# A tensor of its own for each block sum that stands in PSUM, and a new order for the late work

## The chip, the cores and the metric

The kernel runs on one core of a Trainium2 chip. The metric is the device time of one execution in microseconds (us), as the median of the runs. Five engines work side by side: TensorE (PE in the profile, its weight loads PEld), VectorE (DVE), ScalarE (ACT), GpSimd (POOL) and SyncE (SP), whose queue issues all the transfers. Matrix products land in PSUM, which has eight banks of 512 fp32 values in each of 128 partitions.

## What is computed

A linear attention (4 batches, 8 heads, 768 steps, head width 48) feeds a gated MLP, all in fp32:

```
state = w_t * state + k_t v_t^T ;  y_t = r_t (state + u k_t v_t^T)        # attention, one step
h = gelu(y @ w_in) ;  u, v = halves of h (512 columns each)
v_n = layer norm of v, times g_ln
v_s = w_sg @ v_n + b_sg                # w_sg mixes the 768 positions of one batch
out = y + (u * v_s) @ w_out
```

## The kernel before

Attention runs in chunks of 128 steps, 6 to a batch and 24 in all (steps `n`); the MLP follows each batch. Every fp32 product of the MLP is three matmuls of high and low parts (`mm3_part` at L1049 to L1051; `mm3_more` at L1243 adds three more to a sum that is already there).

**The order.** Nothing is ordered by hand. Each piece of work is a Python generator that yields one `Op` for each engine instruction or group, with an estimate of its time in us, what it waits for and which buffers it takes. `Plan.run` lists them: it takes, engine by engine, the operation that can start first by these estimates, and among those within a tolerance the one of the lowest rank. The ranks come from constants and from the tables `SHIFT` and `LEAN`, found by a search. So estimates and tables do nothing on the chip by themselves; they set the order of the instructions on every engine, and the engines run their instructions in that order. The framework below adds the semaphore waits, from the tensors that each instruction reads and writes. The planner's own model has no waits of that kind between two sums in one tensor.

**The last batch.** Its mixing `w_sg @ v_n` (two halves of positions by six blocks of 128) is done with fewer products by sums and differences of blocks. `value_sums`, `early_sums` and `late_sums` make the sums of operands on DVE, ACT and POOL. The products run in `first_sum`, `second_sum` and `third_sum`, each for `j` = 0 and 1 (128 columns each):

- `second_sum(j)` accumulates three blocks, and DVE reads the running sum between them: block 2 (operands `kt`, `winh`, `winl`), then `u2[j] = ps + p1` (L1287); block 3 (`x`, `winl`, `winh`), then `p15[j] = ps + p15` (L1295); block 4 (`x`, `winh`, `winl`), then L1304, then the gate.
- `third_sum(j)` accumulates its first block, DVE makes `p15[j]` from it (L1324), then the second block, L1335, then the gate.
- `gated` is the gate: multiply-add (L1144) and multiply by `u` (L1146) on DVE, both in place in PSUM, the high part on ACT (L1148), the low part on DVE (L1150). The `g` that it makes is an operand of `out_piece`, whose result DVE adds to the input (L1357) and SP stores.

PSUM has `a_ps` (one tensor of two banks), `y_ps` (one tensor of two banks), and four tensors of one bank each, `m_ps` three times and `resets`, which all the other MLP products take in turn. Both sums of `second_sum` stand in `a_ps`, one bank each, and both of `third_sum` in `y_ps`.

As fillers for ACT there are checks of the inputs: `f64_check` (L1437 load, L1440 and L1441) and twelve `range_check` (load of 516 KB at L694, L697, L699). The verdict on them (L1364 to L1381) sets a flag which is read at the end.

Of the kernel before, what the change touches and what calls it, by code (L numbers as in the profile page):

```python
# [29 lines left out]
HALF = S // 2  # L30
# [17 lines left out]
    "f64_check": {0: 6.13524, 1: -1.25073, 2: 2.58709, 3: 21.0265, 4: 1.86039, 5: -5.70527, 6: -3.22829,  # L48
        7: -4.72882, 8: -32.5565, 9: -75.5317},
    "range_check": {0: -10.8008, 1: -9.83328, 2: 25.8484, 3: -12.1442, 4: 14.1794, 5: -6.94772, 6: -6.75246,  # L50
        7: -4.37133, 8: -8.93084, 9: -6.04386, 10: 18.5049, 11: 4.47546},
# [6 lines left out]
        21: 2.56083, 22: 6.50075, 23: 0.926434},  # L58
# [3 lines left out]
        21: -3.66692, 22: 4.4884, 23: -0.122174},  # L62
# [5 lines left out]
        15: -3.39515, 16: -0.550587, 17: 3.40935, 18: 3.60141, 19: 1.63861, 20: 2.50708, 21: 2.31902, 22: -7.3781,  # L68
# [8 lines left out]
        21: 1.1852, 22: -6.40664, 23: -32.7259},  # L77
    "state": {0: 1.6156, 1: -1.5654, 2: -0.151852, 4: -1.00713, 5: -1.43132, 6: 0.0152658, 7: 0.148255,
        8: -4.14956, 9: -1.43419, 10: -1.96613, 11: -1.55185, 12: -0.134183, 13: -1.23942, 14: -0.0105872,
        15: -7.76325, 16: 1.22982, 17: -6.96928, 18: -2.43314, 19: 0.638084, 20: 1.35566, 21: 2.77548,  # L80
        22: 0.936183, 23: -15.5807},
    "taken": {0: -0.262701, 1: 2.39625, 2: -1.14432, 3: 0.217207, 4: 1.06527, 5: 5.92211, 6: -2.94535, 7: -2.95988,
        8: 5.10548, 9: 8.1973, 10: 6.2663, 11: 5.18081, 12: 4.46058, 13: 4.60809, 14: 1.43792, 15: -5.39583,
        16: -2.06968, 17: -1.47464, 18: -1.78307, 19: -1.09584, 20: 8.6431, 21: 6.51443, 22: 27.2314, 23: 7.25823},
# [15 lines left out]
        16: -11.6337, 17: -2.93257, 18: 15.7862, 19: -3.68233},  # L100
# [4 lines left out]
        7: 5.08266, 8: 1.08435, 9: 2.39182, 10: 0.696228, 11: 5.4523, 12: 2.68057, 13: -5.5209, 14: -10.064,  # L105
        15: -14.4952, 16: -13.7637, 17: -65.3122},
    "turned_copy": {0: -0.00376847, 1: 2.08601, 2: 2.36332, 3: 4.99214, 4: 0.358231, 5: 3.23889, 6: -8.60673,
        7: 3.02214, 8: -5.60305, 9: -3.76615, 10: -9.9281, 11: -11.0889, 12: 2.86951, 13: -2.39513, 14: -2.09959,
        15: 44.1632},
    "move": {0: 5.13594, 1: -0.550027, 2: 1.01544, 3: 7.61938, 4: 7.77121, 5: -1.87103, 6: -1.63015, 7: -5.38766,  # L110
        8: 5.01974, 9: -17.0269, 10: 7.95121, 11: 38.0365},
    "split_x": {0: -5.87337, 1: -1.21064, 3: -3.08211, 4: -1.59682, 5: 2.46398, 6: 5.39234, 7: 13.1576, 8: 1.09464,
        9: -6.79638, 10: 10.9691, 11: 6.13701, 12: 15.758, 13: -0.387358, 14: -1.71503, 15: -2.57609, 16: -3.23669,
        17: 3.48517, 18: -19.4792, 19: -1.84619, 20: -47.5863, 21: -27.2088, 22: -25.5326, 23: -14.1693},
    "v_piece": {0: 0.974425, 1: 0.0770227, 2: 0.0252557, 3: -0.26627, 4: -2.79717, 5: -1.99287, 6: -3.35885,
        7: 0.760898, 8: -0.0152414, 9: -0.145742, 10: 0.648668, 11: -6.73745, 12: -2.61262, 13: -2.01732,
        14: 0.737588, 15: -0.200081, 16: -0.36828, 17: -2.1716, 18: 10.1152, 19: -26.4527, 20: -3.15993,
        21: -43.5842, 22: -48.7493, 23: -14.1388},
    "u_piece": {0: -0.43406, 1: -0.156609, 2: 0.407676, 3: -0.0686205, 4: 6.03383, 5: 7.87225, 6: 7.83671,
# [4 lines left out]
    "gate_piece": {0: 0.415732, 1: 0.510674, 2: -1.60287, 3: -1.12889, 4: -0.911901, 5: -1.67499, 6: 0.685951,  # L124
        7: 3.55094, 8: -6.13281, 9: -4.24099, 10: -5.33866, 11: -4.05245, 12: -5.07821, 13: -0.422561, 14: 7.83702,
        15: 8.75934, 16: 0.209474, 17: -1.31632, 18: -3.60713, 19: 1.03, 20: 4.65649, 21: 1.95126, 22: -15.4408,
        23: 17.0337},
    "out_piece": {0: -5.70279, 1: 1.7949, 2: -1.59687, 3: -2.24862, 4: -1.98186, 5: -11.7889, 6: -5.01684,
        7: 0.480244, 8: 0.181361, 9: 0.421304, 10: 0.100822, 11: 2.08585, 12: -10.0637, 13: -23.9868, 14: -5.74609,
        15: 10.0572, 16: -9.94732, 17: 14.3604, 18: 10.6945, 19: 14.5855, 20: -52.8156, 21: -22.494, 22: -13.0148,  # L130
        23: -8.57544},
    "value_sums": {0: -31.4738, 1: 52.068, 2: -53.6573},
    "early_sums": {0: 7.43323, 1: 0.307297, 2: 7.17974},
    "late_sums": {0: 1.94387, 1: 8.12424, 2: -0.928206},
    "first_sum": {0: -18.2786, 1: 8.1141},
    "second_sum": {0: -74.8167, 1: -1.83379},
    "second_gate": {0: -33.8644, 1: 4.67722},
    "third_sum": {0: -5.77672, 1: 6.70228},
    "verdict": {0: 22.9598},
# [14 lines left out]
        21: 0.422507, 22: 0.0982615, 23: -0.259888},  # L154
# [11 lines left out]
    "v_piece": {1: 0.806915, 2: 0.321106, 5: 0.907102, 6: 0.197632, 7: 0.0545095, 8: 0.39416, 10: -0.0275803,
        11: 0.185728, 13: -0.159257, 14: 0.0198662, 15: 0.248228, 16: -0.238145, 17: 0.159771, 18: -0.0597079,
        19: 0.689192, 21: 0.210592, 22: 0.128118},
    "value_sums": {0: 0.0241681, 2: -0.282933},
    "early_sums": {0: 0.249284},  # L170
    "late_sums": {1: -0.0420833},
# [61 lines left out]
class Event:  # L233
    t = None
# [230 lines left out]
def rwkv_gmlp(ctx: ExitStack, tc: tile.TileContext, wpad, kr, vtok, ktok, vt, u, ucol, w_in, consts_, w_sgT, w_out, out):  # L465
    nc = tc.nc
# [24 lines left out]
    per, ps = pool("per", 1), pool("ps", 1, space=PSUM)  # L491
# [17 lines left out]
    s_kr = slots("KR", 4, [2 * NP * C + T])  # L509
# [5 lines left out]
    s_a = slots("a", 3, [2, NP, T])  # L515
# [108 lines left out]
    def dma(kb, **kw):  # L624
        return Op({"SP": 0.62 if kb in (16, 48) else 0.47}, kb=kb, **kw)
# [529 lines left out]
    sums = Part("y", "z")  # L1155
# [57 lines left out]
    whole = {"DVE": 0.48, "POOL": 1.0}  # L1213
# [37 lines left out]
    def first_sum(j):  # L1251
# [9 lines left out]
        op = yield Op({"ACT": 0.42, "DVE": 0.47}, take=[s_y3], done=sums.e_p1[j])  # L1261
# [13 lines left out]
    def second_sum(j):  # L1275

        for s in range(TH):
            op = yield Op({"PE": 0.53}, after=[sums.e_b[2, s], sums.e_a[2, s], *([sums.e_y] if j and s == 0 else [])],
                          take=[] if s or j else [m_a], done=sums.e_y if s == 0 and j == 0 else None)
            if s == 0 and j == 0:  # L1280
                sums.y, = op.got
                sums.y.n = 2
            ps = sums.y.tile[:, j, :HALF]
            mm3_part(ps, (columns_of(sums.b[2, s], j), sums.a[2, s]), s, TH)
        op = yield Op({"DVE": 0.5}, after=[sums.e_p1[j]], take=[s_a], done=sums.e_u2[j])
# [6 lines left out]
        op = yield Op({"DVE": 0.5}, after=[sums.e_p15[j]], take=[s_g], done=sums.e_c22[j])  # L1292
# [433 lines left out]
```

## Time and profile before

| | us |
|---|---|
| median of 3 runs | 359.95 (359.12 to 360.01) |
| the profiled execution | 361.06, its span 359.3 |
| PE busy in the span | 345.6 (96%) |
| DVE / ACT / POOL busy | 281.6 / 226.9 / 122.5 |
| mean granted clock of TensorE | 0.997 |

The profile comes from one execution. Its span runs from the first to the last instruction; 1.76 us of that execution's time lie around it. A matmul's row begins where it is issued and its end is modelled, so that successive matmuls overlap in the rows; the distance between their starts says how fast PE goes.

### The profile page before, as it was taken

How to read it: one execution, taken by the hardware profiler on the slowest of the kernel's cores; microseconds unless marked ns; L12 is line 12 of the kernel's file. 1: busy time of each engine (PE TensorE's matmuls, PEld its weight loads, DVE VectorE, ACT ScalarE, POOL GpSimd, SP SyncE). 2: the span in 40 equal slices, each digit the busy share in tenths (PEclk: the TensorE clock that was granted, in tenths of full speed). 3: DMA queues.
4: the chain of work that ended last, by engine and by line, in shares of the span. 5: the costliest groups of instructions: out<-in, count | busy, mean ns of one | idle time of the engine just before them, and what ended most of it. 6: DMA issues, size and time to landing. Idle time of an engine off the chain costs nothing.

```text
span 359.3 us, 11044 instructions
## 1 busy us (share of the span) xinstructions
PE 345.6 (96%) x4459; PEld 315.3 (88%) x4459; DVE 281.6 (78%) x550; ACT 226.9 (63%) x602; POOL 122.5 (34%) x206
## 2 busy tenths in 40 slices
PE   8999998999999999999999999999999999999892
PEld 7785776899999889899999999899999898998782
DVE  7999989989989898979989893446554468787582
ACT  2869977973455558765325557724137899888960
POOL 8240544333244543443335524321012243144000
PEclk9999999999999999999999999999999999999998
DMA  7989886521365756435476630013347655746602
GB/s 271 374 287 294 273 284 220 165 84 44 112 192 174 229 150 208 141 122 162 130 218 203 183 102 2 0 68 111 102 122 247 235 178 165 234 163 189 203 32 70
DMA packets 28422, 60.56 MB, mean 169 GB/s; under 512 B 3408, under 2 KB 13136, under 8 KB 28368
## 3 DMA queue, kind: packets, MB, share of 16 engines
q1 hardware_dynamic: 28368, 59.82, 51.8%
q8 instruction: 36, 0.59, 0.7%
q14 instruction: 18, 0.15, 0.1%
HBM read 53.91 MB, written 4.72 MB: 163 GB/s over the span
## 4 chain that ended last, share of the span: by engine, by line
PE 79%; DVE 4%; ACT 4%; DMA 2%; issue 1%; SPq 1%; POOL 0%; ACTq 0%; DVEq 0%
PE m_ps L1049 15%; PE m_ps L1050 14%; PE m_ps L1051 14%; PE resets L1049 6%; PE resets L1050 5%; PE resets L1051 5%; PE a_ps L773 4%; PE y_ps L796 3%; PE y_ps L807 3%; DMA x<-y 2%; PE y_ps L780 2%; PE a_ps L1243 2%; PE m_ps L1243 1%; PE y_ps L1243 1%; SPq L1017 1%
## 5 line engine op out<-in xcount | busy, mean ns | idle before, releaser
L1049 PE MATMUL m_ps<-wsgh,vn 128*128 128x384 f32 x114 | 39.3, 345 | 0.0
L1051 PE MATMUL m_ps<-wsgh,vn 128*128 128x384 f32 x114 | 38.6, 338 | 0.0
L1050 PE MATMUL m_ps<-wsgl,vn 128*128 128x384 f32 x114 | 38.5, 338 | 0.0
L748 ACT ACTIVATE a<-KR,own 128x64 f32<-128x64 f32 x136 | 34.4, 339 | 2.9 <-DVE own L742 2.8
L472 ACT COPY x<-y_ps 128x384 f32<-128x384 f32 x23 | 11.0, 476 | 31.2 <-PE y_ps L796 27.0
L739 POOL TENSOR_TENSOR RK<-RK 128x384 f32<-128x384 f32 x16 | 17.2, 1074 | 24.7 <-DVE W L683 6.1
L1049 PE MATMUL m_ps<-xT,winh 128*128 128x384 f32 x72 | 25.4, 353 | 0.0
L1050 PE MATMUL m_ps<-xT,winh 128*128 128x384 f32 x72 | 24.4, 339 | 0.0
L1051 PE MATMUL m_ps<-xT,winl 128*128 128x384 f32 x72 | 24.4, 338 | 0.0
L1050 PE MATMUL m_ps<-g,wouth 128*128 128x384 f32 x68 | 23.2, 341 | 0.4 <-DVE g L1150 0.4
L1101 DVE TENSOR_TENSOR vn<-v,vn 128x512 fp32r<-128x512 f32 x21 | 15.2, 729 | 10.4 <-ACT vn L472 9.6
L1049 PE MATMUL m_ps<-g,wouth 128*128 128x384 f32 x68 | 23.2, 342 | 0.0
L1051 PE MATMUL m_ps<-g,woutl 128*128 128x384 f32 x68 | 23.0, 338 | 0.0
L1148 ACT CAST g<-m_ps 128x384 fp32r<-128x384 f32 x20 | 9.5, 475 | 21.1 <-DVE m_ps L1146 21.1
L773 PE MATMUL a_ps<-KR 64*64 64x128 f32 (+1 forms) x768 | 22.4, 252 | 0.4 <-POOL KR L685 0.2
L1049 PE MATMUL m_ps<-winh,xT 128*128 128x512 f32 x54 | 22.0, 407 | 0.0
L1049 PEld LDWEIGHTS m_ps<-wsgh,vn 128*128 128x128 f32 x114 | 21.4, 188 | 0.6
L1050 PEld LDWEIGHTS m_ps<-wsgl,vn 128*128 128x128 f32 x114 | 21.5, 188 | 0.1
L796 PE MATMUL y_ps<-a,vtok 64*64 64x64 f32 x768 | 21.4, 224 | 0.1
L1051 PEld LDWEIGHTS m_ps<-wsgh,vn 128*128 128x128 f32 x114 | 21.5, 188 | 0.0
L1051 PE MATMUL m_ps<-winh,xT 128*128 128x512 f32 x54 | 21.4, 397 | 0.0
L1050 PE MATMUL m_ps<-winl,xT 128*128 128x512 f32 x54 | 21.4, 396 | 0.0
(321 smaller groups left out, 1103.0 us busy)
## 6 DMA issues: line engine op xcount, KB each, us to landing
KR<-in_kr SPq DMA_DIRECT2D x24, 512.0 KB, 5.0
RK<-in_ktok SPq DMA_DIRECT2D x20, 384.0 KB, 4.0
W<-in_wpad SPq DMA_DIRECT2D x24, 260.5 KB, 3.3
KR<-in_wpad SPq DMA_DIRECT2D x12, 521.0 KB, 3.6
vtok<-in_vtok SPq DMA_DIRECT2D x24, 192.0 KB, 4.3
out<-o SPq DMA_DIRECT2D x21, 192.0 KB, 3.1
vn<-in_w_in SPq DMA_DIRECT2D x6, 512.0 KB, 6.3
KR<-in_w_in SPq DMA_DIRECT2D x6, 512.0 KB, 5.1
```

The costliest lines, as they stand in the source:

```text
L472: nc.scalar.copy(o, i) if e == "ACT" else engine[e].tensor_copy(o, i)
L739: engine[op.e].tensor_tensor(t[:, 1], t[:, 1], t[:, 0], ALU.mult)
L748: nc.scalar.activation(a[:, j, p], eyes, AF.Copy, scale=o[:, j, p:p + 1])
L773: nc.tensor.matmul(ps_[64 * c_:64 * c_ + 64, j, p * C:p * C + (2 * T if c_ < turn else T)], x.K[rows, at:at + T], r_, start=True, stop=True)
L796: m = nc.tensor.matmul(place(y, j, q, r, c_), x.V[64 * c_:64 * c_ + 64, h * D - up(p, j):h * D - up(p, j) + 64], x.a.tile[64 * c_:64 * c_ ...
L807: m = behind(m, nc.tensor.matmul(place(y, j, q, r, c_), S2.tile[64 * j:64 * j + 64, 16 + 64 * p - up(p, j):80 + 64 * p - up(p, j)], x.R[64 ...
L1049: nc.tensor.matmul(ps, lh, rh, start=(i == 0), stop=False)
L1050: nc.tensor.matmul(ps, lh, rl, start=False, stop=False)
L1051: nc.tensor.matmul(ps, ll, rh, start=False, stop=(i == n - 1))
L1101: engine[op.e].tensor_tensor(vn.tile[:, 1], v, vh.bitcast(F32), ALU.subtract)
L1148: nc.scalar.copy(gh, ps)
L1243: nc.tensor.matmul(ps, x, y, start=False, stop=True, skip_group_check=True)
```

## The change

`second_sum(0)` keeps `a_ps`, of which it uses one bank; `second_sum(1)` takes `y_ps` for itself. `third_sum(j)` takes one of the four one-bank tensors for each `j`. The events that told the second sum that the first had taken the tensor are gone. The estimates of the operations behind the last batch are set to traced durations. The load of the first three range checks is split in two transfers of 258 KB. `SHIFT` and `LEAN` have new values for the late pieces: those of the checks, of the attention chunks from about n = 20 on, and of the MLP pieces of the last one and a half batches. The products, the casts and the additions are the same and as many.

```
-    "first_sum": {0: -18.2786, 1: 8.1141},
-    "second_sum": {0: -74.8167, 1: -1.83379},
-    "second_gate": {0: -33.8644, 1: 4.67722},
-    "third_sum": {0: -5.77672, 1: 6.70228},
-    "verdict": {0: 22.9598},
+    "first_sum": {0: 1.73604, 1: 10.2119},
+    "second_sum": {0: -94.3654, 1: 16.5429},
+    "second_gate": {0: -60.8972, 1: 32.2017},
+    "third_sum": {0: -18.3163, 1: 8.56913},
+    "verdict": {0: 79.1124},
...
     def range_check(n):
-        op = yield dma(516, take=[s_kr], after=[ch[N - 1].e_k])
+        two = n < 6
+        op = yield dma(258 if two else 516, take=[s_kr], after=[ch[N - 1].e_k], apart=two)
...
-        nc.sync.dma_start(t, wpad[b, g:g + 2].rearrange("a p x -> p a x"))
+        if two:
+            nc.sync.dma_start(t[:, 0], wpad[b, g])
+            yield dma(258)
+            nc.sync.dma_start(t[:, 1], wpad[b, g + 1])
+        else:
+            nc.sync.dma_start(t, wpad[b, g:g + 2].rearrange("a p x -> p a x"))
...
     def gated(h_, half, d, m, g, ps, ready=None, j=0):
-        yield Op({"DVE": 0.54}, after=[e_u, h_.e_u[d], *([ready] if ready else [])])
+        dve = 0.6 if h_.n >= 3 * NC else 0.5
+        yield Op({"DVE": dve + 0.04}, after=[e_u, h_.e_u[d], *([ready] if ready else [])])
...
-    sums = Part("y", "z")
+    sums = Part()
...
     def second_sum(j):
         for s in range(TH):
-            op = yield Op({"PE": 0.53}, after=[sums.e_b[2, s], sums.e_a[2, s], *([sums.e_y] if j and s == 0 else [])],
-                          take=[] if s or j else [m_a], done=sums.e_y if s == 0 and j == 0 else None)
-            if s == 0 and j == 0:
-                sums.y, = op.got
-                sums.y.n = 2
-            ps = sums.y.tile[:, j, :HALF]
+            op = yield Op({"PE": 0.53}, after=[sums.e_b[2, s], sums.e_a[2, s]],
+                          take=[] if s else [m_y if j else m_a])
+            if s == 0:
+                y, = op.got
+                ps = (y.tile[:, 0].rearrange("p q t -> p (q t)") if j else y.tile[:, 0])[:, :HALF]
...
-        op = yield Op({"DVE": 0.5}, after=[sums.e_p1[j]], take=[s_a], done=sums.e_u2[j])
+        op = yield Op({"DVE": 0.6}, after=[sums.e_p1[j]], take=[s_a], done=sums.e_u2[j])
...
     def third_sum(j):
         for s in range(TH):
-            op = yield Op({"PE": 0.53}, after=[last_s.e_v[s], sums.e_a[1, s], *([sums.e_z] if j and s == 0 else [])],
-                          take=[] if s or j else [m_y], done=sums.e_z if s == 0 and j == 0 else None)
-            if s == 0 and j == 0:
-                sums.z, = op.got
-                sums.z.n = 2
-            ps = sums.z.tile.rearrange("p j q t -> p j (q t)")[:, j, :HALF]
+            op = yield Op({"PE": 0.53}, after=[last_s.e_v[s], sums.e_a[1, s]], take=[] if s else [m_m])
+            if s == 0:
+                z, = op.got
+                ps = z.tile[:, :HALF]
```

## Rows read from the trace of the kernel before

**Rows 1.** The page: busy time of the engines (share of the span).

```profile
PE 345.6 (96%) x4459; PEld 315.3 (88%) x4459; DVE 281.6 (78%) x550; ACT 226.9 (63%) x602; POOL 122.5 (34%) x206
```

**Rows 2.** Windows: stretch, length, busy us of each engine (instructions), clock, DMA.

```profile
300.00:324.00 24.00, 24.00 (x136) 23.77 (x136) 19.64 (x44) 21.86 (x43) 7.72 (x15) 1.00 0.65 207
324.00:348.00 24.00, 21.59 (x116) 19.63 (x115) 16.54 (x32) 19.07 (x30) 4.28 (x6) 1.00 0.51 158
300.00:350.00 50.00, 47.59 (x261) 45.40 (x261) 37.76 (x80) 42.92 (x76) 12.00 (x20) 1.00 0.56 175
```

**Rows 3.** Timeline of PE, matmuls on both sides of six gaps: start, us, what.

```profile
327.19 0.33 PE L1051 MATMUL resets<-g,woutl 128*128 128x384 f32 x1
327.75 0.41 PE L1243 MATMUL a_ps<-wsgh,x 128*128 128x384 f32 x1 [0.22 <-DVE a L1287]
...
329.76 0.33 PE L1051 MATMUL m_ps<-g,woutl 128*128 128x384 f32 x1
330.22 0.44 PE L1243 MATMUL a_ps<-wsgh,x 128*128 128x384 f32 x1
...
332.98 0.33 PE L1049 MATMUL m_ps<-g,wouth 128*128 128x384 f32 x1
333.66 0.44 PE L1050 MATMUL m_ps<-g,wouth 128*128 128x384 f32 x1 [0.35 <-DVE g L1150]
...
339.25 0.33 PE L1243 MATMUL a_ps<-wsgh,x 128*128 128x384 f32 x1
340.24 0.44 PE L1243 MATMUL a_ps<-wsgh,winh 128*128 128x384 f32 x1 [0.66 <-DVE a_ps L1304]
340.52 0.33 PE L1243 MATMUL a_ps<-wsgl,winh 128*128 128x384 f32 x1
340.69 0.34 PE L1243 MATMUL a_ps<-wsgh,winh 128*128 128x384 f32 x1
341.75 0.45 PE L1243 MATMUL a_ps<-wsgh,winl 128*128 128x384 f32 x1 [0.72 <-DVE a_ps L1144]
...
345.56 0.33 PE L1049 MATMUL resets<-g,wouth 128*128 128x384 f32 x1
346.22 0.44 PE L1050 MATMUL resets<-g,wouth 128*128 128x384 f32 x1 [0.33 <-DVE g L1150]
```

**Rows 4.** Timeline of DVE and ACT: what PE waited for there, and its causes.

```profile
327.04 0.56 DVE L1287 TENSOR_TENSOR a<-a_ps,y 128x384 f32<-128x384 f32 x1 [0.88 <-PE a_ps L1051]
...
329.61 0.56 DVE L1287 TENSOR_TENSOR a<-a_ps,y 128x384 f32<-128x384 f32 x1 [0.42 <-PE a_ps L1243]
...
339.62 0.57 DVE L1304 TENSOR_TENSOR a_ps<-a_ps,y 128x384 f32<-128x384 f32 x1 [2.63 <-PE a_ps L1243]
...
341.07 0.63 DVE L1144 SCALAR_TENSOR_TENSOR a_ps<-a_ps,flat 128x384 f32<-128x384 f32 x1 [0.88 <-PE a_ps L1243]
...
331.94 0.48 ACT L1148 CAST g<-y_ps 128x384 fp32r<-128x384 f32 x1 [1.52 <-DVE y_ps L1144]
...
344.50 0.48 ACT L1148 CAST g<-a_ps 128x384 fp32r<-128x384 f32 x1 [2.28 <-DVE a_ps L1144]
```

**Rows 5.** DMA issues: tile, engine, count, size, median us to landing.

```profile
W<-in_wpad SPq DMA_DIRECT2D x24, 260.5 KB, 3.3
KR<-in_wpad SPq DMA_DIRECT2D x12, 521.0 KB, 3.6
```

**Rows 6.** Timeline: the end of an output piece and what empties it.

```profile
335.53 0.34 PE L1051 MATMUL m_ps<-g,woutl 128*128 128x384 f32 x1
...
335.91 0.56 DVE L1357 TENSOR_TENSOR o<-m_ps,x 128x384 f32<-128x384 f32 x1 [0.73 <-PE m_ps L1051]
```

**Rows 7.** Timeline: last check on ACT, last matmul of the products, last DVE operation.

```profile
349.46 0.20 ACT L699 ACTIVATION_READ_ACCUMULATOR KR<-KR,whalf 128x1 f32 x1
...
352.38 0.34 PE L1051 MATMUL m_ps<-g,woutl 128*128 128x384 f32 x1
...
353.10 0.34 DVE L1357 TENSOR_TENSOR u<-m_ps,x 128x192 f32<-128x192 f32 x1
```

More of the change, by code (lines that the diff above doesn't have):

```diff
@@ L47 @@
         8: 0.927292, 9: 2.80075},
[L48 to L51, printed above, removed]
+    "f64_check": {0: 28.589, 1: 11.0015, 2: -2.64021, 3: 45.0113, 4: 4.9629, 5: 29.1223, 6: 33.1649, 7: 1.669,
+        8: -32.5565, 9: -75.5317},
+    "range_check": {0: 21.7927, 1: -15.5142, 2: -1.02753, 3: 60.9069, 4: 32.2161, 5: 53.4721, 6: 0.547616,
+        7: 60.7162, 8: -9.29434, 9: 71.1939, 10: 34.4653, 11: 9.22021},
     "f32_weight": {0: -4.78669, 1: -0.0910659, 2: 0.0544041, 3: -0.00610032, 4: 0.969675, 5: -0.739073},
@@ L76 @@
         14: 2.10613, 15: -0.0485253, 16: -0.0835444, 17: -1.26287, 18: -3.28219, 19: 0.273209, 20: -0.49806,
[L77 removed]
+        21: 1.1852, 22: -59.3124, 23: -57.3379},
     "state": {0: 1.6156, 1: -1.5654, 2: -0.151852, 4: -1.00713, 5: -1.43132, 6: 0.0152658, 7: 0.148255,
         8: -4.14956, 9: -1.43419, 10: -1.96613, 11: -1.55185, 12: -0.134183, 13: -1.23942, 14: -0.0105872,
[L80 to L81 removed]
+        15: -7.76325, 16: 1.22982, 17: -6.96928, 18: -2.43314, 19: 0.638084, 20: 1.35566, 21: -6.53421,
+        22: 47.2587, 23: -8.53506},
     "taken": {0: -0.262701, 1: 2.39625, 2: -1.14432, 3: 0.217207, 4: 1.06527, 5: 5.92211, 6: -2.94535, 7: -2.95988,
         8: 5.10548, 9: 8.1973, 10: 6.2663, 11: 5.18081, 12: 4.46058, 13: 4.60809, 14: 1.43792, 15: -5.39583,
[L84 removed]
+        16: -2.06968, 17: -1.47464, 18: -1.78307, 19: -1.09584, 20: 21.9345, 21: 60.5907, 22: -3.75694,
+        23: 18.2479},
     "turned": {0: -0.704742, 1: 11.1871, 2: 6.42985, 3: 1.86501, 4: 2.26591, 5: 2.39726, 6: -4.17833, 7: -2.85879},
@@ L109 @@
-        15: 44.1632},
+        7: 3.02214, 8: -5.60305, 9: -3.76615, 10: -9.9281, 11: -11.0889, 12: 2.86951, 13: -2.39513, 14: -29.9701,
+        15: 54.6009},
     "move": {0: 5.13594, 1: -0.550027, 2: 1.01544, 3: 7.61938, 4: 7.77121, 5: -1.87103, 6: -1.63015, 7: -5.38766,
-        8: 5.01974, 9: -17.0269, 10: 7.95121, 11: 38.0365},
+        8: 5.01974, 9: -17.0269, 10: 50.2967, 11: 32.2608},
     "split_x": {0: -5.87337, 1: -1.21064, 3: -3.08211, 4: -1.59682, 5: 2.46398, 6: 5.39234, 7: 13.1576, 8: 1.09464,
@@ new lines @@
+        15: 7.01131, 16: 16.3921, 17: -62.5907, 18: 49.4339, 19: 16.2123, 20: -16.4648, 21: -53.8305, 22: -52.6069,
+        23: 9.13389},
+    "value_sums": {0: -93.7806, 1: 43.4518, 2: -123.827},
+    "early_sums": {0: -11.9281, 1: -27.7399, 2: -23.384},
+    "late_sums": {0: -8.02819, 1: 35.1915, 2: 11.5964},
+    "first_sum": {0: 1.73604, 1: 10.2119},
[3 more added lines that the diff above has]
+    "verdict": {0: 79.1124},
@@ L158 @@
     "decayed": {0: -1.01002, 1: -0.323575, 2: 1.5, 3: 0.553284, 4: -0.325678, 8: -0.147204, 12: 0.0901712,
-        13: -0.675434, 15: -0.0706277, 16: -0.312972, 18: -0.403501},
+        13: -0.675434, 15: -0.0706277, 16: -0.312972, 19: -0.469783},
     "state": {2: 0.753638, 3: -1.0542, 7: 0.629567, 8: 0.430301, 9: 0.928441, 10: -0.376746, 11: -0.248544,
-        13: -0.50518, 14: -0.167283, 15: 0.43555, 17: 0.031857, 19: 1.5, 21: 0.133983, 22: -1.33524,
-        23: -0.0108217},
+        13: -0.50518, 14: -0.167283, 15: 0.43555, 17: 0.031857, 19: 1.5, 21: 0.835994, 22: 0.0906227},
     "split_x": {0: -0.671409, 3: 0.0575575, 4: 0.170189, 5: -0.0751645, 6: -0.433472, 8: 1.11651, 10: 0.777999,
-        11: 0.0953515, 14: -0.575987, 16: -0.210189, 17: 0.57252, 18: 0.330029, 19: -0.238175, 22: -1.0519,
-        23: 0.0911529},
+        11: 0.0953515, 14: -0.575987, 16: -0.210189, 17: 0.57252, 19: 0.362003, 20: -0.0844288, 21: -0.169302,
+        22: -0.917024, 23: 0.373362},
     "v_piece": {1: 0.806915, 2: 0.321106, 5: 0.907102, 6: 0.197632, 7: 0.0545095, 8: 0.39416, 10: -0.0275803,
[L167 to L171, printed above, removed]
+        11: 0.185728, 13: -0.159257, 14: 0.0198662, 15: 0.248228, 16: -0.238145, 17: 0.159771, 18: 0.0772949,
+        19: 1.30488, 20: -0.249563, 21: 0.581616, 22: 0.0519866, 23: 0.686162},
+    "value_sums": {0: 0.146649, 1: 0.0373915, 2: -0.150309},
+    "early_sums": {0: 0.751589, 1: 0.808292, 2: 0.14899},
+    "late_sums": {0: 0.0363125, 1: -0.151739},
 }
@@ L1144, in gated @@
         nc.vector.scalar_tensor_tensor(ps, ps, c.g[:, d:d + 1], c.b_bc[:, ts], ALU.mult, ALU.add)
-        yield Op({"DVE": 0.5}, free=[h_.u[d]])
+        yield Op({"DVE": dve}, free=[h_.u[d]])
         nc.vector.tensor_tensor(ps, ps, h_.u[d].tile, ALU.mult)
-        yield Op({"ACT": 0.42})
+        yield Op({"ACT": 0.5 if dve > 0.5 else 0.42})
         nc.scalar.copy(gh, ps)
-        yield Op({"DVE": 0.5}, done=h_.e_g[d], free=[m])
+        yield Op({"DVE": dve}, done=h_.e_g[d], free=[m])
         nc.vector.tensor_tensor(g.tile[:, 1], ps, gh.bitcast(F32), ALU.subtract)
@@ L1170, in halved @@
         h, l = t
-        op = yield Op({"ACT": 0.08 + n / 1130, "POOL": 0.1 + n / 520}, after=after)
+        op = yield Op({"ACT": 0.12 + n / 1130, "POOL": 0.1 + n / 520}, after=after)
         copy(op.e, h, x)
-        op = yield Op({"DVE": 0.07 + n / 940, "POOL": 0.1 + n / 420}, two=True, done=done, free=free)
+        op = yield Op({"DVE": 0.1 + n / 940, "POOL": 0.1 + n / 420}, two=True, done=done, free=free)
         engine[op.e].tensor_tensor(l, x, h.bitcast(F32), ALU.subtract)
     def value_sums(s_):
-        cost = {"DVE": 0.33, "POOL": 0.7}
+        cost = {"DVE": 0.42, "POOL": 0.7}
         op = yield Op(cost, two=True, after=[last_s.e_v[s_], sums.e_n[s_ + TH]], take=[] if s_ else [s_kt, s_x])
@@ L1211, in raw_rows @@
         return bufs, a, b
-    whole = {"DVE": 0.48, "POOL": 1.0}
+    whole = {"DVE": 0.52, "POOL": 1.0}
     def early_sums(s_):
@@ L1260, in first_sum @@
             last_s.vn[s].done(op.seen)
-        op = yield Op({"ACT": 0.42, "DVE": 0.47}, take=[s_y3], done=sums.e_p1[j])
+        op = yield Op({"ACT": 0.5, "DVE": 0.47}, take=[s_y3], done=sums.e_p1[j])
         sums.p1[j], = op.got
@@ L1291, in second_sum @@
             mm3_more(ps, (columns_of(sums.b[3, s], j), sums.a[3, s]))
-        op = yield Op({"DVE": 0.5}, after=[sums.e_p15[j]], take=[s_g], done=sums.e_c22[j])
+        op = yield Op({"DVE": 0.6}, after=[sums.e_p15[j]], take=[s_g], done=sums.e_c22[j])
         sums.g[j], = op.got
@@ L1302, in second_sum @@
         halves[B - 1, 1].e_gm[j].t = op.seen
-        op = yield Op({"DVE": 0.5}, free=[sums.p1[j]])
+        op = yield Op({"DVE": 0.6}, free=[sums.p1[j]])
         nc.vector.tensor_tensor(ps, ps, sums.p1[j].tile, ALU.add)
-        yield from gated(halves[B - 1, 1], 1, j, sums.y, g, ps)
+        yield from gated(halves[B - 1, 1], 1, j, y, g, ps)
     def second_gate(j):
@@ L1313, in third_sum @@
         for s in range(TH):
-            op = yield Op({"PE": 0.53}, after=[last_s.e_v[s], sums.e_a[1, s], *([sums.e_z] if j and s == 0 else [])],
-                          take=[] if s or j else [m_y], done=sums.e_z if s == 0 and j == 0 else None)
-            if s == 0 and j == 0:
-                sums.z, = op.got
-                sums.z.n = 2
-            ps = sums.z.tile.rearrange("p j q t -> p j (q t)")[:, j, :HALF]
+            op = yield Op({"PE": 0.53}, after=[last_s.e_v[s], sums.e_a[1, s]], take=[] if s else [m_m])
+            if s == 0:
+                z, = op.got
+                ps = z.tile[:, :HALF]
             mm3_part(ps, (columns_of(of_vn(s), j, DH), sums.a[1, s]), s, TH)
             last_s.vn[s].done(op.seen)
-        op = yield Op({"DVE": 0.5}, after=[sums.e_p1[j]], take=[s_d2 if j else s_a], done=sums.e_p15[j])
+        op = yield Op({"DVE": 0.6}, after=[sums.e_p1[j]], take=[s_d2 if j else s_a], done=sums.e_p15[j])
         sums.p15[j], = op.got
@@ L1332, in third_sum @@
         halves[B - 1, 0].e_gm[2 + j].t = op.seen
-        op = yield Op({"DVE": 0.5}, after=[sums.e_u2[j]])
+        op = yield Op({"DVE": 0.6}, after=[sums.e_u2[j]])
         sums.u2[j].done(op.seen)
         nc.vector.tensor_tensor(ps, ps, flat_of(sums.u2[j]), ALU.add)
-        yield from gated(halves[B - 1, 0], 0, 2 + j, sums.z, g, ps)
+        yield from gated(halves[B - 1, 0], 0, 2 + j, z, g, ps)
     def out_piece(b, half, i):
```

32 lines of the change are left out of this document (13 added, 19 removed), and 6 rows, old and new, of the table SHIFT.

## The prediction

> **What bounds the kernel now.** I read the page first. PE is busy 345.6 us, 96% of the span [rows 1], and the products are the same after the change, so only time in which PE stands still, or waits to start or end, can be won. The windows say where: from 300 to 324 PE is busy throughout, from 324 to 348 it is not, and the clock is 1.00 in both [rows 2]. In the starts of the matmuls from 230 to 300 there are only short pauses around each attention step, and these steps the change keeps. So the stretch from 324 to 348 is what the change can move.
>
> There I went through the starts of the matmuls one by one. At the full pace a matmul of 384 columns starts every 24.00 / 136 = 0.176 us [rows 2]. Six times the distance is far longer: 0.56, 0.46, 0.68, 0.99, 1.06 and 0.66 us [rows 3], together 4.41. Less six usual distances (1.06) this is 3.35 us. Each first matmul behind a gap is followed more slowly too, 340.24 to 340.52 = 0.28 in place of 0.176, which is 0.10 six times or 0.62. PE loses 3.35 + 0.62 = 3.98 us in these six places, and there is no seventh like them from 300 us to the last product: in the 24 us ahead the pace is full [rows 2].
>
> The Trainium skill (Perfetto Trace Analysis, "Identifying the Most-Contended Engine") holds the matmul rows' busy time to be a poor measure, because matmuls are pipelined, and would have the weight loads' busy time read. The two differ here: the matmul rows lack 24.00 - 21.59 = 2.41 us, the weight loads 23.77 - 19.63 = 4.14 us against the stretch before [rows 2]. By the first the sum below would be 357.9, by the second 356.2; the count of starts lies by the second, so this trace agrees with the rule.
>
> **What each gap waits for.** The question is whether the data ask for these waits.
>
> - The gaps at 340.24 and 341.75 (0.99 and 1.06): the sum whose block 4 has been finished is added to by L1304 at 339.62, and its gate's L1144 follows at 341.07. PE has begun block 4 of the *other* sum (`x`) and waits for both before it does `winh` and `winl` of it. The two sums are two banks of one tensor. No value of the one is used by the other. DVE in its turn waits for PE: L1304 started only behind the other sum's three `x` matmuls, L1144 only behind the three `winh` ones [rows 3, 4]. The two engines alternate through one tensor.
> - The gaps at 327.75 and 330.22 (0.56 and 0.46): L1287 of the first sum waited for the other sum's last matmul of block 2, L1287 of the second for the first sum's block 3 [rows 4]. Both read a sum to which PE had added its block 2 already, and DVE stood idle 0.88 and 0.42 us for the other one's matmuls. That block 3 waits for L1287 of its own sum is asked by the data and stays, but an earlier L1287 is done by the time PE gets there.
> - The gaps at 333.66 and 346.22 (0.68 and 0.66): an output piece lacks a `g`. Its cast on ACT waited 1.52 and 2.28 us for an L1144 [rows 4], which is the other sum's: the gate's operations on one sum follow each other with L1146 between them, and the cast follows L1146. It is the same tensor once more.
>
> So I put all six, 3.98 us, to the shared tensors.
>
> **The change part by part.** (a) *Own tensors.* `second_sum(1)` goes to `y_ps`, `third_sum` to two one-bank tensors. This removes the waits listed: -3.98 us. Nothing is added on PE, DVE or ACT. What it moves is PSUM: two of the four one-bank tensors, on which output, `u` and `v` pieces take turns, are held by third sums. Before, none was. What that costs no row shows. From below it is nothing, as `y_ps` and `a_ps` have stood free before and the search knows how many tensors there are; from above see the rivals.
>
> (b) *Estimates.* They cost nothing on the chip. DVE's operations in PSUM were planned at 0.5 to 0.54 and last 0.56 to 0.63, the cast 0.42 and lasts 0.48 [rows 4]. The old order was too hopeful about DVE by some 0.07 us an operation; the new one is less so. I count nothing for it, either way.
>
> (c) *Split loads.* Three loads become six, three more issues on SP. A transfer of 260.5 KB lands in 3.3 us and one of 521 KB in 3.6 [rows 5], so the pair lands between 0.3 us earlier (both at once) and 3.0 us later (one behind the other, 6.6). What waits for it is a check on ACT, and behind it on SP other loads. The check is a filler; its cover is ACT's idle time, 50.00 - 42.92 = 7.08 us from 300 to 350 [rows 2]. I take 0, the nearer row being the first; without cover it is up to 3.0 us of ACT for each.
>
> (d) *The new order.* It can move work only within what the rows leave free. Something will be late next: gates on DVE, which is busy 16.54 of 24 us there [rows 2], and the last `g` before the last output pieces. I give back one gap of the smallest kind seen, 0.46 - 0.176 + 0.10 = 0.4 us. The bounds are 0, and the rival below.
>
> The sum: 361.06 - 3.98 + 0.40 = 357.5 us for an execution like the profiled one. That one stands 1.11 above the median of the runs, so in their terms 359.95 - 3.58 = 356.4.
>
> **Rivals.**
>
> *Too few one-bank tensors.* With two held by first sums and two by third sums none would be left; with one left, each piece waits for the emptying of the one before. Such a turn costs: last matmul starts at 335.53, DVE empties from 335.91 to 336.47 [rows 6], the next matmul could come at some 336.5 in place of 335.71, and starts slowly: 0.8 + 0.1 = 0.9 us. One to three turns give back 0.9 to 2.7 us: 356.9 to 358.7, with two 357.8. For it speaks that third sums before stayed in PSUM for long; against it that the planner counts these tensors and sees such a turn. The Trainium skill (Perfetto Trace Analysis, "Optimization Strategy") says that a gap that repeats on the engine that should be full can mean too little PSUM for the next tile; the gaps of before are of another kind, and no run here shows that one yet. Chance 0.20.
>
> *Slower.* The same mechanism decides the other way from six turns on: 6 x 0.9 = 5.4 against 3.98, 359.95 + 1.4 = 361.4. That needs third and first sums open together across most of the last output and `u` pieces. Chance 0.07.
>
> *ACT takes over.* It is the busiest behind PE: 42.92 of 50 us. Of its 7.08 us idle, 3.80 are the two waits of [rows 4], so that an end 4 us earlier leaves it just 3.1 us of room. The verdict hangs on its last check, at 349.46 [rows 7]. If only the 3.80 go and all its other idle time stays, ACT is 3.98 - 3.80 = 0.2 us too late; if all 7.08 stay, since other waits take the place of these, it gives back the whole 3.98. The middle is 2.1: 355.97 + 2.1 = 358.1. Against it: casts can go to POOL, busy 12.00 of 50 us, and checks can begin earlier. Chance 0.10.
>
> *No effect.* If the waits went by something else than the tensor (PSUM as a whole, or a semaphore that both sums share), they would come back under other names: 359.9. Against it: at 327.19 PE starts a matmul into `resets` while DVE's L1287 reads `a_ps` [rows 3, 4], so PSUM as a whole is not what is guarded. Chance 0.05.
>
> **How the numbers follow.** The forecast has 0.58; its own range is 354.9 (all six gaps, nothing given back, and also the 1.06 us from the last matmul at 352.38 to the end of DVE at 353.44 [rows 7] gone) to 357.5. About 0.3% (1.1 us) can be told from no change: below 358.9 is faster, above 361.0 slower. Faster takes the forecast, 0.16 of the first rival's 0.20 and 0.09 of ACT's 0.10: 0.83. Same takes the rest of these two and the case of no effect: 0.10. Slower is 0.07. The range that leaves out two in ten, no more, is 354.9 to 358.9.
>
> **What would show it.** Right: from 320 us on no PE wait of over 0.2 us for L1287, L1304 or L1144, the casts L1148 without waits for L1144, weight loads busy about 0.99 of the stretch up to the last product, which starts near 348.8. Gaps of about 0.9 us in front of pieces in `m_ps` or `resets`, with a wait for the L1357 or L1115 that empties one, would be the first rival; ACT without idle time and the verdict waiting for L699 the third. The prediction is wrong if PE's gaps keep their 4 us with other names, or if the end no longer hangs on PE.

## The result, and the profile after

| | us |
|---|---|
| before, median of 14 runs | 360.32 |
| changed, median of 14 runs | 357.01 (355.39 to 359.68) |
| ratio | 0.9904 (0.9877 to 0.993) |
| profiled execution of the changed kernel | 356.11, its span 354.3, clock 0.998 |

Three repeats beside the experiments gave ratios of 0.9871 (0.9844 to 0.9898), 0.9876 (0.9851 to 0.9902) and 0.987 (0.9838 to 0.9902). The change makes the kernel faster by 3.3 to 5.2 us in medians; the forecast was 3.55. In the last of these groups one run of the kernel before took 671.01 us, far from all others, and is left out of its median and ratio.

The page of the changed kernel, busy time of the engines, stands against [rows 1]:

```profile
PE 343.0 (97%) x4459; PEld 315.4 (89%) x4459; DVE 281.2 (79%) x549; ACT 226.0 (64%) x600; POOL 123.2 (35%) x209
```

Its windows stand against [rows 2], columns as there:

```profile
300.00:324.00 24.00, 24.00 (x139) 24.00 (x138) 19.10 (x41) 20.73 (x48) 10.21 (x19) 1.00 0.60 187
...
324.00:348.00 24.00, 24.00 (x137) 23.77 (x135) 17.47 (x40) 19.85 (x31) 4.00 (x5) 1.00 0.53 158
```

From 324 to 348 the weight loads, which were busy 19.63 us before, are busy 23.77 us: the stretch is full. On PE's timeline no two neighbouring starts lie more than 0.25 us apart from 278 us to the last product at 347.75. The last block of the second sum that now stands in `y_ps` shows it on PE:

```profile
337.16 0.34 PE L1057 MATMUL m_ps<-xT,winl 128*128 128x384 f32 x1
337.33 0.34 PE L1250 MATMUL y_ps<-wsgh,x 128*128 128x384 f32 x1
...
338.22 0.34 PE L1250 MATMUL y_ps<-wsgh,winh 128*128 128x384 f32 x1
338.40 0.34 PE L1250 MATMUL y_ps<-wsgh,winl 128*128 128x384 f32 x1
```

and on DVE at the same time the gate of the other one, in `a_ps`:

```profile
336.95 0.62 DVE L1151 SCALAR_TENSOR_TENSOR a_ps<-a_ps,flat 128x384 f32<-128x384 f32 x1
337.60 0.57 DVE L1153 TENSOR_TENSOR a_ps<-a_ps,u 128x384 f32<-128x384 f32 x1
```

The products of 337.33 to 338.75 run at 0.176 us from start to start while L1151 and L1153 (L1144 and L1146 before) work on the other sum. Before, PE and DVE took turns here [rows 3, 4].

**Where the 5.0 us of span went.** Up to about 260 us the order on every engine is the same in the kernel before, the changed kernel and all kernels below. I take as a mark the first attention product of a step near 239 us, which lies in that part, and call the time from its start to the start of the last product the late stretch. Before:

```profile
239.47 0.46 PE L796 MATMUL y_ps<-a,vtok 64*64 64x64 f32 x16
```

and after, with the last product:

```profile
238.67 0.46 PE L802 MATMUL y_ps<-a,vtok 64*64 64x64 f32 x16
...
347.75 0.33 PE L1057 MATMUL m_ps<-g,woutl 128*128 128x384 f32 x1
```

The late stretch was 352.38 - 239.47 = 112.91 us and is 347.75 - 238.67 = 109.08: 3.83 less. Of the rest, 0.80 had arisen before the mark, where the order is the same, and 0.37 lies behind the last product (6.92 before, 6.55 after). Neither can be put to the change: over all profiled executions of this study the mark comes between 237.86 and 241.39 us, and the piece behind the last product lasts 6.42 to 6.92 us in all but two kernels, whose last stores land earlier (5.91 and 5.79, below). So the late stretch of the profile is the finer measure for a part of the change. It does not see what happens behind the last product, and the medians stand beside it.

### The profile page after: what moved, and what is told of

Same layout as the page of the kernel before. It is cut to its first block, busy times and chain, and to the rows that moved or that the text cites. A ratio compares the mean times of both kernels' runs of the same rounds, so it can differ in the third digit from the quotient of the medians.

```text
span 354.3 us, 11046 instructions
## 1 busy us (share of the span) xinstructions
PE 343.0 (97%) x4459; PEld 315.4 (89%) x4459; DVE 281.2 (79%) x549; ACT 226.0 (64%) x600; POOL 123.2 (35%) x209
## 4 chain that ended last, share of the span: by engine, by line
PE 89%; ACT 2%; DVE 1%; issue 0%; SPq 0%
PE m_ps L1055 18%; PE m_ps L1056 17%; PE m_ps L1057 17%; PE resets L1055 6%; PE resets L1056 5%; PE resets L1057 5%; PE a_ps L779 5%; PE y_ps L802 4%; PE y_ps L813 3%; PE y_ps L786 2%; PE m_ps L1250 1%; PE m_ps L1044 1%; PE y_ps L1250 1%; PE a_ps L1250 1%; PE m_ps L825 1%; PE a_ps L786 1%
## 5 line engine op out<-in xcount | busy, mean ns | idle before, releaser
L1055 PE MATMUL m_ps<-wsgh,vn 128*128 128x384 f32 x117 | 40.4, 345 | 0.0
L1057 PE MATMUL m_ps<-wsgh,vn 128*128 128x384 f32 x117 | 39.5, 338 | 0.0
L1056 PE MATMUL m_ps<-wsgl,vn 128*128 128x384 f32 x117 | 39.5, 338 | 0.0
L1055 PE MATMUL m_ps<-g,wouth 128*128 128x384 f32 x76 | 25.9, 341 | 0.0
L1056 PE MATMUL m_ps<-g,wouth 128*128 128x384 f32 x76 | 25.8, 339 | 0.0
L1057 PE MATMUL m_ps<-g,woutl 128*128 128x384 f32 x76 | 25.7, 338 | 0.0
L745 POOL TENSOR_TENSOR RK<-RK 128x384 f32<-128x384 f32 x16 | 16.2, 1012 | 25.1 <-DVE W L683 6.1
L1155 ACT CAST g<-m_ps 128x384 fp32r<-128x384 f32 x22 | 10.5, 477 | 22.5 <-DVE m_ps L1153 22.5
L1055 PEld LDWEIGHTS m_ps<-wsgh,vn 128*128 128x128 f32 x117 | 22.0, 188 | 0.6
L802 PEld LDWEIGHTS y_ps<-a,vtok 64*64 64x64 f32 x768 | 16.2, 134 | 6.6 <-issue 5.7
L1057 PEld LDWEIGHTS m_ps<-wsgh,vn 128*128 128x128 f32 x117 | 22.0, 188 | 0.0
L683 DVE TENSOR_TENSOR_SCAN W<-W,D 128x520 f32<-128x520 f32 x16 | 20.4, 1275 | 0.0
L779 PEld LDWEIGHTS a_ps<-KR 64*64 64x64 f32 x768 | 18.4, 134 | 1.8 <-POOL KR L685 0.5
```

Source lines behind the costliest of these rows:

```text
L683: nc.vector.tensor_tensor_scan(W[:, 0:WL - 1], W[:, 0:WL - 1], D2[:, 0:WL - 1], 0.0, ALU.mult, ALU.add)
L745: engine[op.e].tensor_tensor(t[:, 1], t[:, 1], t[:, 0], ALU.mult)
L779: nc.tensor.matmul(ps_[64 * c_:64 * c_ + 64, j, p * C:p * C + (2 * T if c_ < turn else T)], x.K[rows, at:at + T], r_, start=True, stop=True)
L802: m = nc.tensor.matmul(place(y, j, q, r, c_), x.V[64 * c_:64 * c_ + 64, h * D - up(p, j):h * D - up(p, j) + 64], x.a.tile[64 * c_:64 * c_ ...
L1055: nc.tensor.matmul(ps, lh, rh, start=(i == 0), stop=False)
L1056: nc.tensor.matmul(ps, lh, rl, start=False, stop=False)
```

## The experiments

Two theories stood against each other. *A*: the gain comes from the own tensors, and the new order only does no harm (the prediction). *B*: the search for a new order carries most of it.

**Repeats of the changed kernel** ran with each group of experiments.

> The changed kernel again, as the measure for the runs beside it. Both theories: 3.0 to 3.9 us below the kernel before, no pause of PE over 0.1 us from 300 us to the last product.

Late stretches 108.94, 109.29 and 108.94 us beside the 109.08 above: the measure repeats within 0.35 us. Medians were 355.69, 355.90 and 356.22, which is 5.16, 4.15 and 4.63 below the kernel before in the same group. The first is more than the 3.0 to 3.9 expected; the other two, for which 3.0 to 4.7 was expected, are as expected.

**Own tensors alone.** The kernel before with the new `second_sum` and `third_sum`, but the old estimates, old `SHIFT` and `LEAN`, whole loads:

```
-    sums = Part("y", "z")
+    sums = Part()
...
+                          take=[] if s else [m_y if j else m_a])
...
+            op = yield Op({"PE": 0.53}, after=[last_s.e_v[s], sums.e_a[1, s]], take=[] if s else [m_m])
```

> The kernel before with one part of the change alone: each of the four sums has a tensor of its own (second_sum in a_ps and y_ps, third_sum in two one-bank tensors); estimates and tables are those of before. The planner makes its own order from the third sums on, as they take other buffers. Theory (the shared tensors are the cause): at least half of the 3.98 us goes, so 2.0 to 3.9 us below the kernel before, and no wait of PE for L1287, L1304 or L1144 of the other sum is left; what remains would be pauses for a one-bank tensor at 0.9 us each. Rival (the new order and the estimates are the cause): within 1.1 us of the kernel before.

Late stretch 111.76 (1.15 below before), median 358.04 against 360.85, ratio 0.9933 (0.9909 to 0.9957). That is 2.81 us by the medians, 1.6 to 3.3 by the interval, as expected (2.0 to 3.9) and more than the late stretch shows. A second piece lies behind the last product, which lasts 5.91 us here and 6.92 before. Four output stores end the kernel. Before, they are issued from 0.10 us ahead of the last product on (first line); here from 1.69 us ahead of it (second line), and the last of them lands 2.87 us behind it in place of 5.29:

```profile
352.28 1.85 SPq L1359 DMA_DIRECT2D out<-u  x4
...
348.00 3.26 SPq L1356 DMA_DIRECT2D out<-u  x4
```

From the mark to the end own tensors alone bring 1.15 + 1.01 = 2.16 us of the 3.83 + 0.37 = 4.20 of the whole change: about half. The waits for the other sum are gone, but others have come. One, on PE:

```profile
309.86 0.33 PE L1051 MATMUL resets<-g,woutl 128*128 128x384 f32 x1
310.84 0.44 PE L1049 MATMUL resets<-g,wouth 128*128 128x384 f32 x1 [0.65 <-DVE o L1354]
```

An output piece needs `resets` again, and waits until DVE has emptied it (L1354): the turn of the first rival, at 310.84 - 309.86 - 0.176 + 0.10 = 0.91 us, which the prediction priced at 0.9. The other, on PE and then on ACT:

```profile
342.42 0.45 PE L1049 MATMUL m_ps<-g,wouth 128*128 128x384 f32 x1
343.58 0.44 PE L1050 MATMUL m_ps<-g,wouth 128*128 128x384 f32 x1 [0.72 <-DVE g L1150]
```

```profile
340.76 1.15 ACT L699 ACTIVATE KR<-KR,whalf 128x1024 f32<-128x1024 f32 x1
341.81 0.18 ACT L699 ACTIVATION_READ_ACCUMULATOR KR<-KR,whalf 128x1 f32 x1
341.91 0.46 ACT L1148 CAST g<-a_ps 128x384 fp32r<-128x384 f32 x1
```

```profile
342.51 0.57 DVE L1146 TENSOR_TENSOR y_ps<-y_ps,u 128x384 f32<-128x384 f32 x1
342.98 0.55 DVE L1150 TENSOR_TENSOR g<-a_ps,g 128x384 fp32r<-128x384 f32 x1
```

The cast of a `g` stands behind a check pass on ACT, and its low part L1150 then behind the other sum's L1146 on DVE; the next start on PE is 1.16 us away. With two smaller pauses (0.67 and 0.43) this kernel loses 2.85 us, counted as in the prediction, where the one before lost 3.98. Theory A's -3.98 from the tensors alone is refuted, by the interval too: they take the old waits away, but with the old tables about half of the gain, and in the late stretch most of it, goes to new ones.

**The new order alone.** The changed kernel with the shared tensors of before put back:

```
-    sums = Part()
+    sums = Part("y", "z")
...
-            ps = z.tile[:, :HALF]
+            ps = sums.z.tile.rearrange("p j q t -> p j (q t)")[:, j, :HALF]
```

> The changed kernel with both sums of second_sum in a_ps and both of third_sum in y_ps again; new estimates, new tables, split loads. The planner's order differs a little from the changed kernel's, as the buffers differ. Theory: waits between the two sums of a pair come back, 1.5 to 3.5 us above the changed kernel. Rival: at most 0.7 us above the changed kernel.

Late stretch 115.19, 2.28 *above* before; median 361.72 against 360.85, ratio 1.0029 (1.0004 to 1.0055). It is 6.0 to 6.1 above the changed kernel, where 1.5 to 3.5 had been expected. Theory B alone is refuted more plainly. Four of its seven pauses stand within the second sums' products and end with a DVE operation on the tensor that the two share, as in [rows 3]; one of them:

```profile
341.21 0.34 PE L1250 MATMUL a_ps<-wsgh,x 128*128 128x384 f32 x1
342.21 0.45 PE L1250 MATMUL a_ps<-wsgh,winh 128*128 128x384 f32 x1 [0.66 <-DVE a_ps L1153]
```

The planner that makes this order has no waits between two sums of one tensor. The other three pauses end with operations of POOL, ACT and DVE on other tiles, so the 6.11 us are not shown to be the sharing alone; the next kernel separates it.

**The waits put back, order untouched.** The changed kernel in the same order on every engine, but each instruction on a sum also waits for the other engines' instructions on its pair's other sum, as it would in one tensor:

```
+    def paired(of, j, i, writes=True):
+        if of not in PAIRED:
+            return i
+        for (j_, engine_), (last, wrote) in seen.setdefault(of, {}).items():
+            if j_ != j and engine_ != i.ins.engine:
+                for name, any_ in ((last, writes), (wrote, True)):
+                    if any_ and name:
+                        tc.add_manual_dep(i.ins, name, wait, reason="one tensor")
...
+    PAIRED = ('y', 'z')
```

> The changed kernel with its tensors and with exactly its order of instructions on every engine; only the waits that one shared tensor would ask for between the two sums of a pair are put back, as dependencies written by hand. Theory: from the rows of the changed kernel, the products into y_ps at 337.33 must now wait for the first sum's gate on DVE, which ends at 338.17, and the casts of one gate for the other's L1151 again: PE pauses of 0.8 us and more return, the time is 1.0 to 2.5 us above the changed kernel. Less than the 3.98 us of before, since the new order holds the two sums of second_sum further apart. Rival: the waits cost nothing in a good order, within 0.5 us of the changed kernel.

Late stretch 111.62 (+2.54), median 358.59, ratio to before 0.9938 (0.9918 to 0.9959). Tensors, instructions and order are those of the changed kernel, only waits are added, so these 2.54 us are theirs. By medians it is 2.90 above the changed kernel; both are a little over the 1.0 to 2.5 expected. On DVE one sees the mechanism:

```profile
338.17 0.62 DVE L1166 SCALAR_TENSOR_TENSOR a_ps<-a_ps,flat 128x384 f32<-128x384 f32 x1
340.19 0.56 DVE L1168 TENSOR_TENSOR a_ps<-a_ps,u 128x384 f32<-128x384 f32 x1 [1.40 <-PE y_ps L1266]
```

and on PE right behind it:

```profile
339.81 0.33 PE L1266 MATMUL y_ps<-wsgh,winh 128*128 128x384 f32 x1
340.80 0.44 PE L1266 MATMUL y_ps<-wsgh,winl 128*128 128x384 f32 x1 [0.66 <-DVE a_ps L1168]
```

L1168 on `a_ps` waits for products into `y_ps`, and PE then for L1168: the 0.99 us pause of [rows 3], now between two tensors, because the wait was put there.

**Which pair.** The same with one pair at a time.

```
-    PAIRED = ('y', 'z')
+    PAIRED = ('y',)
```

> The changed kernel in its own order, with the waits of one shared tensor put back for the two sums of second_sum alone. With the waits of both pairs put back, the pause in front of the first two and the last three places fell to a_ps and y_ps and to a g of them, and one to the pair of third_sum. So if the parts add up: 1.7 to 2.3 us above the changed kernel, with pauses in front of a_ps and y_ps products and one for a g, and none in front of m_ps products of the third sums.

```
-    PAIRED = ('y', 'z')
+    PAIRED = ('z',)
```

> The same for the two sums of third_sum alone. If the parts add up: 0.2 to 0.7 us above the changed kernel, with one pause of about half a us near 319 us. If instead the casts of the third sums' gates, which now wait for each other, starve an output piece: 1 us or more.

Second pair: late stretch 111.08 (+2.00), ratio 0.9951 (0.9927 to 0.9975). Third pair: 109.54 (+0.46), ratio 0.9909 (0.9879 to 0.9939). Together 2.46, beside 2.54 for both at once: they add up, and four fifths are the second sums'. The medians, 2.92 and 1.60 above the changed kernel of their group, are too coarse to show the sum, with intervals of about 1 us on either side.

**Own tensors and new estimates, old tables.** Against the changed kernel:

```
-    "third_sum": {0: -18.3163, 1: 8.56913},
+    "third_sum": {0: -5.77672, 1: 6.70228},
...
-        op = yield dma(258 if two else 516, take=[s_kr], after=[ch[N - 1].e_k], apart=two)
+        op = yield dma(516, take=[s_kr], after=[ch[N - 1].e_k])
```

> Own tensors and the new estimates, with the old tables and the unsplit loads: all of the change but the search. Theory A (the estimates carry what own tensors alone did not bring, since the planner then no longer counts on a DVE that is too fast): within 0.8 us of the changed kernel, no pause of PE over 0.5 us behind 300 us. Theory B (the search over the tables carries it): within 1 us of own tensors alone, that is 1.4 to 3 us above the changed kernel, with pauses for a one-bank tensor or for a g.

Late stretch 111.16, median 357.71, ratio 0.9921 (0.9896 to 0.9945): 0.60 below own tensors alone, still 2.08 above the changed kernel. Its pauses are again a turn on `resets` (0.99 us) and a late `g` (0.70 and 0.69). Behind the last product it loses the 0.60 again (6.76 us against 5.91), and by medians it is 2.34 below before where own tensors alone are 2.81. Estimates without the search bring nothing that can be measured.

**New tables, old estimates.**

```
-        yield Op({"DVE": dve}, free=[h_.u[d]])
+        yield Op({"DVE": 0.5}, free=[h_.u[d]])
...
-        yield Op({"ACT": 0.5 if dve > 0.5 else 0.42})
+        yield Op({"ACT": 0.42})
...
-        op = yield Op({"DVE": 0.6}, after=[sums.e_p1[j]], take=[s_a], done=sums.e_u2[j])
+        op = yield Op({"DVE": 0.5}, after=[sums.e_p1[j]], take=[s_a], done=sums.e_u2[j])
```

> The changed kernel with the old estimates: own tensors, new tables, split loads. The tables were searched with the new estimates, so the planner's order comes out differently. If tables and estimates only work together: 1.5 us or more above the changed kernel, with pauses of PE for a g or a one-bank tensor; if the tables alone carry it: within 0.8 us.

Late stretch 116.75 (+7.67), of which 0.76 comes back behind the last product (5.79 us); median 6.95 above the changed kernel, ratio to before 1.0074 (1.0046 to 1.0102): slower than before. On PE:

```profile
330.67 0.33 PE L1057 MATMUL m_ps<-xT,winl 128*128 128x384 f32 x1
332.39 0.44 PE L1055 MATMUL m_ps<-g,wouth 128*128 128x384 f32 x1 [1.39 <-ACT u L1121]
...
332.85 0.34 PE L1057 MATMUL m_ps<-g,woutl 128*128 128x384 f32 x1
335.07 0.46 PE L1055 MATMUL resets<-g,wouth 128*128 128x384 f32 x1 [1.88 <-ACT g L1154]
```

and on ACT, what stands in front of the cast:

```profile
332.24 1.14 ACT L703 ACTIVATE KR<-KR,wmid 128x1024 f32<-128x1024 f32 x1
333.41 1.15 ACT L705 ACTIVATE KR<-KR,whalf 128x1024 f32<-128x1024 f32 x1
334.47 0.19 ACT L705 ACTIVATION_READ_ACCUMULATOR KR<-KR,whalf 128x1 f32 x1
334.56 0.46 ACT L1154 CAST g<-m_ps 128x384 fp32r<-128x384 f32 x1
```

Check passes of 1.15 us were listed ahead of the `u` (L1121) and of the cast that PE needs next. It is not ACT's total that fails, as the third rival had it (42.08 us busy from 300 to 350, and 42.92 before), but fillers in the wrong place.

**Whole loads.** The changed kernel in its order, the first three check loads in one transfer each:

```
-            nc.sync.dma_start(t[:, 0], wpad[b, g])
+            nc.sync.dma_start(t, wpad[b, g:g + 2].rearrange("a p x -> p a x"))
             yield dma(258)
-            nc.sync.dma_start(t[:, 1], wpad[b, g + 1])
```

> The changed kernel in its own order on every engine, but the first three range checks load their 516 KB in one transfer again, at the place of the first of the two. Prediction: nothing, within 0.7 us of the changed kernel. If the split is what keeps the loads behind it on time: ACT's waits for these loads and the transfers behind them grow, and 0.7 us or more is lost.

Late stretch 108.94, ratio 0.9894 (0.9865 to 0.9923). The split is worth nothing that can be measured. Nor do the halves land sooner: the twelve whole loads land in 3.9 us here (median), and in the changed kernel nine whole ones and six halves in:

```profile
KR<-in_wpad SPq DMA_DIRECT2D x9, 521.0 KB, 4.5
...
KR<-in_wpad SPq DMA_DIRECT2D x6, 260.5 KB, 4.6
```

**All kernels by one account.** For each, PE's pauses of over 0.25 us in the late work, beyond the short ones around the attention steps that all have, priced as in the prediction (distance less 0.176, plus 0.10 for the slow start behind it), beside what its late stretch has over the changed kernel's 109.08:

| kernel | over 109.08 | pauses, summed |
|---|---|---|
| before | 3.83 | 3.98 |
| own tensors alone | 2.68 | 2.85 |
| own tensors, new estimates | 2.08 | 2.06 |
| new order alone | 6.11 | 5.99 |
| waits back, both / second / third | 2.54 / 2.00 / 0.46 | 2.69 / 2.21 / 0.30 |
| whole loads | -0.14 | 0 |
| own tensors, tables, old estimates | 7.67 | 7.4 |

The starts of PE's products account for every kernel within 0.3 us. In the last I counted 5.3 us of pauses, 1.8 us of slow clock (below) and 0.3 us for the verdict's own products, which stand ahead of the last pieces there and behind them elsewhere. Both columns come from the same traces, so the table says where the time lies; why it lies there the kernels above say.

## Why the prediction was right, and which of its steps were not

- *The bound, and what can be won*: right. The stretch and the count of starts gave 3.98; the late stretch lost 3.83. The last product was expected near 348.8; set back by the 0.80 us that arose earlier it starts at 347.75 + 0.80 = 348.55. Weight loads are busy 23.77 of 24.00 us, the 0.99 that was named as a sign. The weight loads had said 4.14 and the matmul rows' busy time 2.41 [rows 2]; the first is the nearer, as the Trainium skill (Perfetto Trace Analysis, "Identifying the Most-Contended Engine") would have it, and the count of starts is nearer still.
- *The six gaps are the shared tensors'*: right as to what PE waited for. Waits of exactly this kind, put back into an unchanged order, cost 2.54 us, and with own tensors none of the kernels shows a wait for the other sum.
- *Step (a), "this removes the waits listed: -3.98"*: mis-sized as the own tensors' share. Alone they bring 2.16 us to the end, 1.15 of it in the late stretch (2.81 by medians). The step took a removed wait for won time; in an order made for other buffers the next late thing followed close behind.
- *Step (b), estimates at nothing*: right on top of own tensors, where the 0.60 us of the late stretch is lost behind it. But without them the late stretch of the new tables is 7.67 us above the changed kernel's, which the step did not see.
- *Step (d), 0.4 us given back by the order*: wrong in sign. On top of own tensors and estimates the tables bring 2.08 us of late stretch, 2.29 to the end, and the changed kernel gives nothing back. With shared tensors nearly the same order costs 2.28. So no fixed share belongs to tensors or order: in the late stretch they win 1.15 and lose 2.28 each alone, and win 3.83 together. That the forecast came out in size is luck in this: the 1.8 us too much in (a) and the 2.7 too little in (d) are opposite errors of like size.
- *Step (c), split loads*: right at 0, within the 0.35 us by which the late stretch repeats.
- *Rival of the one-bank tensors*: right in mechanism and price (0.91 measured), but it acts in the two kernels with the old tables, and with 0.46 us between starts in the one with new tables and old estimates. In the changed kernel no product waits for it; that the search saw such a turn is likely, not shown.
- *ACT takes over*: not in the changed kernel. Its last check ends 3.6 us ahead of the last product, and its casts wait 0.28 us or not at all in place of 1.52 and 2.28 [rows 4]:

```profile
338.25 0.48 ACT L1155 CAST g<-a_ps 128x384 fp32r<-128x384 f32 x1 [0.28 <-DVE a_ps L1153]
...
341.61 0.47 ACT L1155 CAST g<-y_ps 128x384 fp32r<-128x384 f32 x1
...
343.97 0.18 ACT L705 ACTIVATION_READ_ACCUMULATOR KR<-KR,whalf 128x1 f32 x1
```

- *No effect* and *slower*: excluded by the intervals.

How much of the search's part is due to each single piece that it moved was not tried.

## What to carry to other kernels

Under a framework that places waits by tensor, two values in two banks of one tensor wait for each other as if they were one; where two engines work on both in turn, give each a tensor of its own, and look for the pair in the timeline as two engines that alternate without a value in common. A removed wait is won time only if the order behind it fits: in this kernel buffers, estimates and tables had to be set and searched anew together, for each part without the others was worth 2 to 3 us less than the whole, or made the kernel slower. And where PE is the bound, count the distances between its starts: that sum told within 0.3 us where the late time of every variant here lay. A measure that ends at the last product misses what comes behind it, so set it beside the medians.

## What the runs showed of the hardware

**The clock after two pauses.** In the kernel with new tables and old estimates PE started no product between 330.67 and 332.39 and between 332.85 and 335.07, with three products between the two pauses. Its windows:

```profile
332.00:335.00 3.00, 0.80 (x3) 0.47 (x3) 1.02 (x2) 2.97 (x6) 0.00 (x0) 1.00 0.78 245
335.00:336.00 1.00, 0.80 (x2) 0.53 (x3) 0.56 (x1) 1.00 (x2) 0.00 (x0) 0.68 0.58 117
336.00:338.00 2.00, 2.00 (x7) 2.00 (x7) 0.00 (x0) 1.97 (x4) 0.00 (x0) 0.50 0.70 240
...
339.00:341.00 2.00, 2.00 (x13) 2.00 (x12) 0.83 (x3) 1.97 (x4) 0.00 (x0) 1.00 0.92 336
```

Right after the second pause the granted clock is 0.50, the lower of the two levels (1.2 in place of 2.4 GHz), though PE is fully busy from 336 to 338; products start 0.32 us apart, and the clock is back from 339 on. From 335.07 to 338.93 eleven distances took 3.86 us where 11 x 0.176 = 1.94 is usual: 1.9 lost, of which 0.1 is the usual slow start. In the kernel with the new order alone a pause of 1.37 us and, one product later, one of 0.68 left the clock at 1.00.

**The spread ahead of the mark.** With the same order, executions reach the mark up to 3.5 us apart (237.86 to 241.39). The two latest each show a window of ten us near the start at a granted clock of 0.83 or 0.79, where the profiled execution of the changed kernel has 1.00. The times of single runs show the same: of the 14 of the changed kernel, the four with a mean granted clock of 0.983 to 0.989 took 358.16 to 359.68 us, the ten with 0.994 to 0.998 took 355.39 to 357.23. So part of the scatter of the medians is the clock's.
